# Attention and a gated layer on one core: eight of twelve column tiles and the last layer by seven-product blocks, with the gated values put into memory

## The chip, the cores and the metric

One core of a Trainium2 chip. The metric is the device time of one execution in microseconds (us), median of several runs.

## The reference, cut to what matters

Eight batches of linear attention (8 heads, 576 tokens, 64 wide, 128 random features) give 4608 tokens of 512 values; a gated layer of 1536 columns follows.

```python
h = x * scale @ omega.T - sq(x * scale) / 2
phi(x) = exp(h - max(h)) / sqrt(128)
num, den = phi(q) @ (phi(k).T @ v), phi(q) @ phi(k).sum()
x = (num / (den + 1e-6)) as [4608, 512]
out = (sigmoid(x @ w_gate) * (x @ w_val)) @ w_out    # 512 -> 1536 -> 512
```

The weights come as float64, in pairs of 32-bit words, and are made into float32 on the chip.

## The kernel before, in words

Matrix products of the gated layer are made exact enough by three passes: each operand is split into a high and a low part (`split`, line 52: ScalarE copies x to the high part, line 54; VectorE or GpSimd subtracts, line 55), and three matmuls, low by high, high by low and high by high, add up in PSUM.

Attention is a list of tasks (norms, keys, queries of a head pair and a batch), six at a time, a step of each in turn (`attention`, line 457). Its last step for a group of tokens is a transpose `pxq` (line 431), a copy to `xs`, and a store to `xT` in memory. `ready(n)` says whether the first n tokens are through.

Weights: `from_float64` (line 58) takes six VectorE operations and a GpSimd add for 384 columns at a time. The first four column tiles of 128 (`first_weights`) are converted and split before the gated layers start; the other eight (`convert_weights`) are converted beside them and put into memory (`w32`), and read back and split after attention (`late_weights`, tiles `w`, `wh`, `wl`).

The gated layers (`passes`, `gated`) are a second stream of pieces that runs beside attention, eight steps of attention per piece. There are two passes over all tokens. The first has four column tiles and chunks of 256 tokens: `gate` and `val` are products of 12 matmuls of 256 columns per tile (line 178, PSUM tiles `gv`), ScalarE takes the sigmoid (204), VectorE multiplies (207, tile `y`), `y` is split into `yh` and `yl`, and 128-token rows of it are multiplied with `w_out` into `acc` (line 192, 512 columns); `acc` is stored to `part`. The second pass has the other eight column tiles and chunks of 512 tokens, so its matmuls on line 178 have 512 columns; at a chunk's end `part` is read and added, and `out` stored.

Instructions are not issued in the order in which the code is written: the tile framework places them on each engine's queue by its own estimates and the code's order. Each queue then runs strictly in order. Matmuls run on PE; DVE is VectorE, ACT ScalarE, POOL GpSimd, SP the engine that issues most loads. Tile pools give each tag a fixed number of buffers, and a pool opened after another has closed takes its space and waits for its last users.

The core of the main loop, which the change rewrites:

```python
while not ready(B * S):
    next(gates)
    credit += RATE          # 8 steps of attention per piece
    while credit >= 1 and not ready(B * S):
        next(steps, None)
        credit -= 1
```

Of the kernel before, what the change touches and what calls it, by code (L numbers as in the profile page):

```python
# [17 lines left out]
M = 128  # L18
# [15 lines left out]
CA, CB = 256, 512   # tokens of a chunk of the gated layers, in their first and second pass  # L34
KC = DM // P
BANK = 512
NJ = DF // P
WP = 384            # weights converted at a time
NE = 4              # column tiles of the first pass
ACTIVE = {"n": 1, "k": 3, "q": 4}  # tasks of attention at a time: norms, keys, queries  # L40
AT_ONCE = 6         # tasks at a time
AHEAD = 8           # tasks to choose from
EVERY = 12          # steps of the first unit's attention per piece of weights
PUT = 5             # pieces of the gated layers per piece of weights
LATE = 3            # the same, once attention is through
# [3 lines left out]
WC = 2 * KC * P + DM   # weights of a column tile: gate, val, out  # L49


def split(nc, hi, lo, x, lo_engine=None):
    """x = hi + lo, both with the mantissa that one pass of the array carries."""
    nc.scalar.activation(out=hi, in_=x, func=AF.Copy)  # L54
    (lo_engine or nc.vector).tensor_tensor(out=lo, in0=x, in1=hi.bitcast(F32), op=ALU.subtract)  # L55
# [12 lines left out]
    # Patterns of positive numbers are in the numbers' order: exponents of -127 to 127 stay.  # L68
# [4 lines left out]
    # The sign and the exponent's highest bit stay in their places, three bits below them go.  # L73
# [7 lines left out]
    # The low word's 32 bits of the mantissa, in units of the number's power of two.  # L81
# [9 lines left out]
def attn_glu_kernel(ctx: ExitStack, tc, qT, kT, qn, kn, va, om, ident, w, out):  # L91
# [6 lines left out]
    w32 = dram.tile([NJ, P, WC], F32, name="w32")  # L98
    part = dram.tile([B * S, DM], F32, name="part")
# [9 lines left out]
    banks = {"at": 8 - 2 - CA // P, "gv": 2, "acc": CA // P}  # L109
# [12 lines left out]
    ws = [None] * NJ  # L122

    def pieces(pool, j):
        for i in range(WC // WP):
            s = slice(i * WP, (i + 1) * WP)
            raw = pool.tile([P, WP, 2], U32, tag="wraw", bufs=2, name=f"wraw{j}_{i}")
            nc.sync.dma_start(out=raw, in_=w[j, :, s, :])
            yield s, from_float64(nc, pool, raw, f"{j}_{i}", WP)

    def weights_of(pool, j):
        ws[j] = [pool.tile([P, WC], F32R, name=f"{n}{j}") for n in ("wh", "wl")]
        return ws[j]

    def first_weights(pool, temps, js):
        """Converts and splits column tiles' weights, a piece a step."""
        for j in js:
            wh, wl = weights_of(pool, j)
            for s, x in pieces(temps, j):
                split(nc, wh[:, s], wl[:, s], x, lo_engine=nc.gpsimd)  # L140
                yield

    def convert_weights(pool, js):
        """Converts column tiles' weights and puts them by, a piece a step."""
        for j in js:
            for s, x in pieces(pool, j):
                nc.sync.dma_start(out=w32[j, :, s], in_=x)
                yield

    def late_weights(pool, js):  # L150
        """Splits column tiles' weights that were put by, a piece a step."""
        n = WC // 2
        for j in js:
            wh, wl = weights_of(pool, j)
            for i in range(2):
                s = slice(i * n, (i + 1) * n)
                x = pool.tile([P, n], F32, tag="w32", bufs=2, name=f"w32_{j}_{i}")
                nc.sync.dma_start(out=x, in_=w32[j, :, s])
                split(nc, wh[:, s], wl[:, s], x)
                yield  # L160

    def gated(pool, C, c, x, js, first):
# [35 lines left out]
        for group in groups:  # L198
            if group is groups[-1]:
                yield True  # L200
# [286 lines left out]
    with tc.tile_pool(name="a", bufs=1, side="right") as pool:  # L487
# [10 lines left out]
        for _ in conv:  # L498
            pass
# [76 lines left out]
```

## Time and profile before

| what | value |
|---|---|
| median of 3 runs | 1295.61 us (1294.84 to 1296.29) |
| span of the profiled execution | 1296.1 us |
| PE busy, share of the span | 96% |
| DVE, ACT, POOL busy | 48%, 40%, 21% |
| bytes moved | 138.12 MB, mean 107 GB/s |
| start of the last `pxq` | 552.9 us |

A row of a group reads: line, engine, operation, output<-inputs, shapes, xcount, then busy us, mean ns of one, and the idle time of the engine before them with what ended it. PE's busy time of one matmul includes its way through the array, and neighbours overlap; what a matmul costs is the distance to the next. In rows of windows stand the stretch, its length, the busy time of each engine with the number of instructions, the granted TensorE clock, the DMA engines' share and GB/s. Rows of the chain of waits give start, length and what held the end then.

### The profile page before, as it was taken

What the parts mean: (1) busy time and instruction counts of PE and PEld (TensorE: products, weight loads), DVE (VectorE), ACT (ScalarE), POOL (GpSimd) and SP (SyncE); (2) the same over time, 40 slices, a digit from 0 to 9 for tenths busy, and PEclk for the clock granted to TensorE, in tenths of its full rate; (3) what the DMA queues carried; (4) which work ended last, traced back from release to release, by engine and by line L of the source; (5) the groups of instructions that cost most, each with busy time, mean ns of one, the idle gap of its engine ahead of it and who ended that gap; (6) DMA issues with size and microseconds to landing.
All of it is one profiled execution on the core that took longest, in us unless ns stands there. A gap on an engine that the chain in (4) does not pass through costs nothing.

```text
span 1296.1 us, 19491 instructions
## 1 busy us (share of the span) xinstructions
PE 1240.6 (96%) x7328; PEld 1077.6 (83%) x7328; DVE 620.0 (48%) x1445; ACT 520.4 (40%) x1119; POOL 276.3 (21%) x304
## 2 busy tenths in 40 slices
PE   5789989999999999999999999999999999999998
PEld 5778989898989988988998878787878787878786
DVE  6989899998988574634111121212121212121212
ACT  6556767676768656544222211112121212121111
POOL 4555253443432323011110100101010101010100
PEclk8779999999999999999999999999999999999999
DMA  8654677676755331154112020202020302020100
GB/s 272 203 178 139 183 228 242 186 241 212 221 174 171 103 119 52 50 178 140 51 49 81 1 98 1 98 1 98 1 98 1 98 1 98 1 98 1 60 6 33
DMA packets 76414, 138.12 MB, mean 107 GB/s; under 512 B 8480, under 2 KB 24096, under 8 KB 76320
## 3 DMA queue, kind: packets, MB, share of 16 engines
q1 hardware_dynamic: 49680, 97.67, 24.5%
q10 hardware_dynamic: 26640, 39.20, 8.8%
q8 instruction: 58, 0.95, 0.3%
q14 instruction: 36, 0.29, 0.1%
HBM read 102.24 MB, written 34.60 MB: 106 GB/s over the span
## 4 chain that ended last, share of the span: by engine, by line
PE 73%; DVE 16%; issue 5%; DMA 4%; ACT 2%; POOL 0%; SPq 0%; DVEq 0%; POOLq 0%; ACTq 0%
PE gv L178 41%; PE acc L192 18%; PE pnq L414 4%; PE pkv L371 4%; PE ptq L402 2%; DVE mxq L328 2%; DMA w<-w 2%; DVE yl L55 1%; DVE hq L391 1%; DVE mxk L328 1%; DVE f64t L78 1%; DMA wraw<-w 1%; DVE subq L389 1%; DVE hmq L331 1%; DVE f64a L84 1%
## 5 line engine op out<-in xcount | busy, mean ns | idle before, releaser
L178 PE MATMUL gv<-xh,wl 128*128 128x256 f32 (+1 forms) x1152 | 394.7, 343 | 1.7 <-POOL wl L55 1.3
L178 PE MATMUL gv<-xl,wh 128*128 128x256 f32 (+1 forms) x1152 | 394.1, 342 | 0.8 <-POOL xl L55 0.8
L178 PE MATMUL gv<-xh,wh 128*128 128x256 f32 (+1 forms) x1152 | 393.4, 342 | 0.0
L207 DVE TENSOR_TENSOR y<-gv,y 128x512 f32<-128x512 f32 x108 | 74.6, 690 | 490.6 <-PE gv L178 439.1
L178 PEld LDWEIGHTS gv<-xh,wl 128*128 128x128 f32 x1152 | 219.4, 191 | 29.8 <-POOL wl L55 1.7
L178 PEld LDWEIGHTS gv<-xl,wh 128*128 128x128 f32 x1152 | 219.3, 190 | 27.9 <-POOL xl L55 1.0
L178 PEld LDWEIGHTS gv<-xh,wh 128*128 128x128 f32 x1152 | 219.3, 190 | 26.7
L55 POOL TENSOR_TENSOR xl<-xr,xh 128x512 fp32r<-128x512 f32 (+1 forms) x76 | 95.6, 1273 | 643.4 <-ACT xh L54 607.4
L192 PE MATMUL acc<-wh,yl 128*128 128x512 f32 x432 | 174.3, 403 | 5.3 <-DVE yl L55 4.9
L204 ACT ACTIVATE y<-gv 128x512 f32<-128x512 f32 x108 | 64.6, 598 | 283.0 <-PE gv L178 262.9
L192 PE MATMUL acc<-wl,yh 128*128 128x512 f32 x432 | 172.7, 400 | 0.0
L192 PE MATMUL acc<-wh,yh 128*128 128x512 f32 x432 | 171.5, 397 | 0.0
L54 ACT ACTIVATE yh<-y 128x512 fp32r<-128x512 f32 x108 | 68.2, 631 | 229.3 <-DVE y L207 228.7
L55 DVE TENSOR_TENSOR yl<-y,yh 128x512 fp32r<-128x512 f32 x108 | 85.2, 789 | 58.9 <-ACT yh L54 58.9
L192 PEld LDWEIGHTS acc<-wh,yl 128*128 128x128 f32 x432 | 81.4, 188 | 27.4 <-DVE yl L55 10.4
L192 PEld LDWEIGHTS acc<-wh,yh 128*128 128x128 f32 x432 | 81.6, 189 | 18.0
L192 PEld LDWEIGHTS acc<-wl,yh 128*128 128x128 f32 x432 | 81.6, 189 | 16.5
L55 POOL TENSOR_TENSOR loq<-rawq,hiq 128x256 fp32r<-128x256 f32 (+1 forms) x80 | 59.4, 753 | 118.5 <-ACT hiq L54 118.4
L363 ACT ACTIVATE kpk<-ppk,nbk 128x128 f32<-128x128 f32 x256 | 72.9, 376 | 25.2 <-DVE nbk L352 22.9
L371 PE MATMUL pkv<-v,kpk 128*128 128x66 f32 x512 | 77.5, 288 | 4.5 <-ACT kpk L363 4.2
L371 PEld LDWEIGHTS pkv<-v,kpk 128*128 128x128 f32 x512 | 71.1, 206 | 8.0 <-ACT kpk L363 7.2
L414 PE MATMUL pnq<-kv,qpq 128*128 128x66 f32 (+1 forms) x640 | 75.8, 272 | 0.2 <-ACT qpq L404 0.2
(66 smaller groups left out, 1679.8 us busy)
## 6 DMA issues: line engine op xcount, KB each, us to landing
wraw<-w SPq DMA_DIRECT2D x48, 384.0 KB, 3.7
xr<-xT SPq DMA_DIRECT2D x68, 256.0 KB, 4.0
v<-va ACTq DMA_DIRECT2D x32, 330.0 KB, 3.9
natk<-kn SPq DMA_DIRECT2D x36, 256.0 KB, 4.4
natq<-qn SPq DMA_DIRECT2D x36, 256.0 KB, 3.7
part<-o ACTq DMA_DIRECT2D x36, 256.0 KB, 2.5
o<-part SPq DMA_DIRECT2D x36, 256.0 KB, 3.5
out<-o ACTq DMA_DIRECT2D x36, 256.0 KB, 3.8
```

The lines of the kernel that those rows point to most:

```text
L54: nc.scalar.activation(out=hi, in_=x, func=AF.Copy)
L55: (lo_engine or nc.vector).tensor_tensor(out=lo, in0=x, in1=hi.bitcast(F32), op=ALU.subtract)
L78: nc.vector.scalar_tensor_tensor(out=t, in0=hi, scalar=0xC0000000, in1=t, op0=ALU.bitwise_and, op1=ALU.bitwise_or)
L178: nc.tensor.matmul(gv[:, g * C : (g + 1) * C], lhsT=a[:, o : o + P], rhs=x[k], start=(m == 0), stop=(m == 3 * KC - 1),)
L192: nc.tensor.matmul(acc[t], lhsT=a[:, s], rhs=b[:, o : o + DM], start=(j == js[0] and m == 0), stop=(j == js[-1] and m == 2),)
L204: nc.scalar.activation(out=y, in_=gate, func=AF.Sigmoid)
L207: nc.vector.tensor_tensor(out=y, in0=val, in1=y, op=ALU.mult)
L328: nc.vector.tensor_reduce(out=mx, in_=pp, axis=AX.X, op=ALU.max)
L363: nc.scalar.activation(out=kp[t][:, h, :], in_=pp[:, 2 * i + h, :], func=AF.Exp, bias=nb[:, i, h : h + 1], scale=SCALE,)
L371: nc.tensor.matmul(pkv[:, h, :], lhsT=kp[b * MID + i][:, h, :], rhs=v[:, i, h, :], start=(i == 0), stop=(i == MID),)
L402: nc.tensor.transpose(out=pt[:, i, :], in_=h_sb[:, i, :], identity=id_sb)
L414: nc.tensor.matmul(pn[r, 2 * i + h, :], lhsT=qp[:, 2 * i + h, r], rhs=kvs[u, p, bb][:, h, :], start=True, stop=True,)
```

## The change

The first pass keeps four plain column tiles (`NE = 4`), now with chunks of 512 tokens (`NC`), and its gated values `y` go to memory (`ye`) without being multiplied with `w_out`. Attention has 12 steps per piece instead of 8, gated pieces begin at 512 tokens ready instead of 256, and one piece of 512 weight columns is converted per two gated pieces.

The other eight column tiles are taken as four pairs, and the products are done by a scheme of seven block products in place of eight: tokens in halves of 256 (Q), inner dimension in halves of two tiles, columns in halves of one tile. The columns `x` get four sums (`operands`: two from loads, four by VectorE and split like the rest, seven in all), and each pair's gate and val weights one `unit` of seven blocks (four from memory, `b`; four differences, `t`, of which VectorE makes each with one subtraction of 256 columns; then two splits, 768 and 1024 columns). `gated` then does for each of two kinds (gate, val) seven products of six matmuls of 256 columns (line 303, PSUM tiles `gw`) into three half-used banks; later products add onto earlier ones in the same bank, after a copy (`p1`) or an add (`u2`, `u3`) has read them. The last two products of a group are issued behind the first three of the next. GpSimd makes the seven operands of the last layer from the four gated blocks (seven operations of 256 columns), and they are stored to `yl`.

The last layer (`last`) comes after all chunks: for each of 18 blocks of 2 x 128 tokens, six pairs are loaded (four of 448 KB from `yl`, two from `ye`, for which VectorE makes the sums), split and multiplied: seven products of three matmuls of 256 columns (line 398, `po`, four banks), then seven adds and two stores. Its six units, n = 8 to 13, are made in the last chunk of the second pass and behind it, through the one buffer tagged `xr`, which the loads of `x` use too.

The diff, cut to its core:

```diff
-CA, CB = 256, 512
+NC = 512
+Q = NC // 2
-RATE = 8
+RATE = 12
+PRODUCT = {1: (0, 0), 2: (1, 1), 3: (6, 2), 4: (2, 6), 5: (3, 3), 6: (4, 4), 7: (5, 5)}
...
+    def unit(pool, n, at=None):
+        if at is None:
+            both = keep.tile([P, KC, NC], F32, tag="xr", bufs=1, name=f"wbt{n}")
+            b, t = both[:, :2], both[:, 2:]
...
+        nc.sync.dma_start(out=b, in_=w32[n])
+        u = pool.tile([P, 2, N_OPS, Q], F32R, tag="u", bufs=UL if pool is late else UE, name=f"u{n}")
+        for o, x, y in (
+            (t[:, 0], b[:, 3], b[:, 0]),
+            (t[:, 2], b[:, 2], b[:, 3]),
+            (t[:, 1], b[:, 2], t[:, 0]),
+            (t[:, 3], b[:, 1], t[:, 1]),
+        ):
+            nc.vector.tensor_tensor(out=o, in0=x, in1=y, op=ALU.subtract)
+        split(nc, u[:, 0, :3], u[:, 1, :3], b[:, :3])
+        split(nc, u[:, 0, 3:], u[:, 1, 3:], t)
...
+    def operands(c):
+        raw = load(c)
...
+        put(0, a11, nc.gpsimd)
+        s1 = combined(3, a21, a22, ALU.add)
+        s2 = combined(4, s1, a11, ALU.subtract)
+        put(4, s2)
+        put(3, s1, nc.gpsimd)
+        put(1, a12)
+        put(6, combined(6, a12, s2, ALU.subtract), nc.gpsimd)
+        put(5, combined(5, a11, a21, ALU.subtract))
+        put(2, a22)
...
+    def gated(c, x, pair, kind, g, y):
...
+        product(1, b0, True)
+        nc.scalar.activation(out=p1, in_=v0, func=AF.Copy)
+        product(6, b1, True)
+        add(u2, v1, p1)
+        product(5, b2, True)
+        yield
+        product(2, b0, False)
...
+        product(7, b1, False)
+        add(u3, v1, p1)
+        add(to[3], v2, u3)
+        yield
+        product(4, b1, False)
+        add(to[2], v1, p1)
+        product(3, b2, False)
+        add(to[1], v2, u2)
...
+    def last(c, s):
+        po = [any_bank(f"po{i}_{id_}") for i in range(4)]
...
+        for j in range(NPAIR):
+            t, n = (("y", 2 * N_OPS), ("g", 8))[j % 2]
+            raw = keep.tile([P, n, P], F32, tag=t, bufs=2, name=f"yr{id_}_{j}")[:, :8]
...
+            split(nc, yh, yl_, raw[:, :N_OPS], nc.gpsimd if j == NPAIR - 1 else None)
+            wh, wl = units[2 * (NPAIR - EP) + j]
+            for n, o in at.items():
+                i, k = PRODUCT[n]
+                for m, (u, v) in enumerate(((yl_, wh), (yh, wl), (yh, wh))):
+                    nc.tensor.matmul(
...
+        late = ctx.enter_context(tc.tile_pool(name="late", bufs=1, side="right"))
+        for n in range(2):
+            unit(late, n, late)
+        first = operands(0)
...
```

How the queues stand now. On PE in the second pass, before (gate and val of one column tile in `gv`, each `x` tile with three matmuls, then the previous tile's `acc`; here the end of one tile's `acc` and the start of the next `gv`):

```order
L192 MATMUL acc_4_3_12865<-wh_8793,yl_7_13019 128x512
L192 MATMUL acc_4_3_12865<-wl_8794,yh_7_13018 128x512
L192 MATMUL acc_4_3_12865<-wh_8793,yh_7_13018 128x512
L178 MATMUL gv_9_0_13079<-xh_8_0_12769,wl_9058 128x512
L178 MATMUL gv_9_0_13079<-xl_8_0_12773,wh_9057 128x512
L178 MATMUL gv_9_0_13079<-xh_8_0_12769,wh_9057 128x512
```

And after, at the turn from chunk 0 to chunk 1 (the names give kind, pair and chunk, then the bank's own number; `xl` is an operand, `u` a unit):

```order
L303 MATMUL gw_0_2_1_8514<-xl_4_8433,u_7582 128x256 x6
L303 MATMUL gw_0_2_1_8515<-xl_3_8436,u_7582 128x256 x6
L303 MATMUL gw_1_5_0_8440<-xl_2_7779,u_8170 128x256 x6
L303 MATMUL gw_1_5_0_8441<-xl_6_7734,u_8170 128x256 x6
L303 MATMUL gw_0_2_1_8513<-xl_1_8495,u_7582 128x256 x6
L303 MATMUL gw_0_2_1_8514<-xl_5_8505,u_7582 128x256 x6
L303 MATMUL gw_1_2_1_8576<-xl_0_8426,u_7594 128x256 x6
L303 MATMUL gw_1_2_1_8577<-xl_4_8433,u_7594 128x256 x6
L303 MATMUL gw_1_2_1_8578<-xl_3_8436,u_7594 128x256 x6
L303 MATMUL gw_0_2_1_8514<-xl_2_8508,u_7582 128x256 x6
```

Groups of six narrow matmuls have taken the place of the wide ones, a bank such as 8514 is written three times, with 18 to 24 matmuls between, and no `acc` stands among them.

On PE at the end of attention, before, around its last `pxq`:

```order
L192 MATMUL acc_0_1_7850<-wh_455,yl_0_7973 128x512
L192 MATMUL acc_0_1_7850<-wl_456,yh_0_7972 128x512
L431 MATMUL pxq_3_7_8206<-id_sb,xq_3_7_8204 128x128 x2
L192 MATMUL acc_0_1_7850<-wh_455,yh_0_7972 128x512
L192 MATMUL acc_0_0_7849<-wh_941,yl_2_8435 128x512
```

And after, 29 rows behind the last `pxq` and on, where chunk 7 of the first pass has just ended; `gv` with `xe_0_7799` is the start of chunk 8:

```order
L303 MATMUL gw_0_2_0_7982<-xl_4_7691,u_7582 128x256
L303 MATMUL gw_0_2_0_7981<-xl_0_7652,u_7582 128x256 x5
L303 MATMUL gw_0_2_0_7983<-xl_3_7694,u_7582 128x256 x6
L303 MATMUL gw_0_2_0_7982<-xl_4_7691,u_7582 128x256 x5
L303 MATMUL gw_0_2_0_7981<-xl_1_7729,u_7582 128x256 x6
L303 MATMUL gw_1_2_0_8035<-xl_4_7691,u_7594 128x256 x6
L303 MATMUL gw_1_2_0_8036<-xl_3_7694,u_7594 128x256 x5
L303 MATMUL gw_0_2_0_7982<-xl_5_7776,u_7582 128x256
L303 MATMUL gw_1_2_0_8036<-xl_3_7694,u_7594 128x256
L303 MATMUL gw_0_2_0_7982<-xl_5_7776,u_7582 128x256 x5
L303 MATMUL gw_0_2_0_7982<-xl_2_7779,u_7582 128x256 x6
L225 MATMUL gv_0_0_7811<-xe_0_7799,wl_111 128x512
```

Before, the first pass simply went on; now the second pass's first products stand on PE ahead of the first pass's last chunk.

On DVE behind attention's last `xq`, before (`wl`: late weights):

```order
L425 TENSOR_TENSOR xq_3_7_8204<-pnq_3_7_8195,invq_3_7_8202 128x256
L55 TENSOR_TENSOR wl_8439<-w_4_0_8440,wh_8438 128x768
L207 TENSOR_TENSOR y_0_8505<-gv_0_1_8507,y_0_8505 128x512
L55 TENSOR_TENSOR wl_8439<-w_4_1_8474,wh_8438 128x768
L55 TENSOR_TENSOR yl_0_8534<-y_0_8505,yh_0_8533 128x512
```

And after, the later part of it (`wt` and `u`: unit 1; `s` and `xl`: operands of second-pass chunk 0 from its load `xr_0_7603`):

```order
L194 TENSOR_TENSOR wt_7592<-wb_7591,wt_7592 128x256
L70 TENSOR_TENSOR u_7594<-wb_7591,u_7594 128x768
L194 TENSOR_TENSOR wt_7592<-wb_7591,wt_7592 128x256
L70 TENSOR_TENSOR xl_4_7691<-s_4_7657,xl_4_7691 128x512
L70 TENSOR_TENSOR xl_1_7729<-xr_0_7603,xl_1_7729 128x512
L264 TENSOR_TENSOR s_6_7732<-xr_0_7603,s_4_7657 128x512
L70 TENSOR_TENSOR u_7594<-wt_7592,u_7594 128x1024
L264 TENSOR_TENSOR s_5_7774<-xr_0_7603 128x512
L284 TENSOR_TENSOR u_2_0_7985<-gw_0_2_0_7982,p_2_0_7984 128x256
L70 TENSOR_TENSOR xl_5_7776<-s_5_7774,xl_5_7776 128x512
L70 TENSOR_TENSOR xl_2_7779<-xr_0_7603,xl_2_7779 128x512
```

The weights' preparation is longer, and the operands that hold `xr` stand behind it.

More of the change, by code (lines that the diff above doesn't have):

```diff
@@ L120, in any_bank @@
         return bank(cycle[-1], name)
[L122 to L133, printed above, removed]
@@ L249, in passes @@
[L249 to L268 removed]
+    ws = {}
@@ new lines, in attn_glu_kernel, with piece, first_weights @@
+    units = {}
+    def piece(pool, i):
+        raw = pool.tile([P, WP, 2], U32, tag="wraw", bufs=2, name=f"wraw{i}")
+        nc.sync.dma_start(out=raw, in_=w[:, i * WP : (i + 1) * WP, :])
+        return from_float64(nc, pool, raw, str(i), WP)
+    def first_weights(pool, temps):
+        n = WE // WP
+        for j in range(NE):
+            ws[j] = wh, wl = [pool.tile([P, WE], F32R, name=f"{t}{j}") for t in ("wh", "wl")]
+            for i in range(n):
+                s = slice(i * WP, (i + 1) * WP)
+                split(nc, wh[:, s], wl[:, s], piece(temps, j * n + i), lo_engine=nc.gpsimd)
+                yield
@@ new lines, in attn_glu_kernel @@
+    tail = ctx.enter_context(tc.tile_pool(name="tail", bufs=1))
+    cycle[:] = ["at", "at", "at", "gv"]
+    n = UL
+    for c, pair in second_pass(x):
+        if n < UL + UE:
+            unit(tail, n, keep)
+            n += 1
+        elif c == NCH - 1 and pair > EP and n < 2 * (NPAIR - EP) + 2 * (pair - EP):
+            unit(late if n < 2 * (NPAIR - EP) + UL else tail, n)
+            n += 1
+    while n < N_LATE:
+        unit(tail, n)
+        n += 1
+    for c in range(NCH):
+        for s in range(Q // P):
+            for _ in last(c, s):
+                pass
```

398 lines of the change are left out of this document (238 added, 160 removed).

## Prediction

> **What bounds the kernel now.** I read the page's totals and slices first, then the windows on both sides of the last attention matmul, then the chain of waits.
>
> ```profile
> span 1296.1 us, 19491 instructions
> PE 1240.6 (96%) x7328; PEld 1077.6 (83%) x7328; DVE 620.0 (48%) x1445; ACT 520.4 (40%) x1119; POOL 276.3 (21%) x304
> PE   5789989999999999999999999999999999999998
> PEclk8779999999999999999999999999999999999999
> ```
>
> TensorE (PE) is busy in nearly every slice, at full granted clock after the first tenth. The reader should see that no other engine is above half. The last attention matmul is a transpose `pxq`; the windows are cut there, for all engines, then for the matmuls of lines 178 and 192 alone:
>
> ```profile
> L431 PE MATMUL pxq<-id_sb,xq x144: 270/273/421, 53.6 to 552.9; 128*128 128x128 f32 x144
> 0.00:553.00 553.00, 506.61 (x3884) 474.99 (x3884) 450.88 (x1221) 362.35 (x866) 214.21 (x257) 0.96 0.56 175
> 553.00:1296.10 743.10, 733.95 (x3447) 602.65 (x3445) 169.15 (x224) 158.09 (x253) 62.06 (x47) 1.00 0.17 56
> 0.00:553.00 553.00, 155.12 (x1056) 136.61 (x1056) 0.96 0.56 175
> 0.00:553.00 553.00, 73.58 (x252) 43.23 (x252) 0.96 0.56 175
> ```
>
> Columns are PE, PEld, DVE, ACT, POOL. Until 553 us attention runs, with PE 92% and VectorE (DVE) 82% busy, so both count. After it PE is 99% busy and DVE 23%. What a matmul really costs there is read from the chain, since busy times of single matmuls overlap (start us, us, what):
>
> ```profile
> 574.98 6.07 DMA w<-w
> 582.94 3.85 DMA w<-w
> 612.66 11.51 PE gv L178 x96
> 692.71 2.79 PE acc L192 x12
> 695.50 5.61 PE gv L178 x24
> 744.75 1.54 DVE yl L55
> 812.67 1.54 DVE yl L55
> 1286.63 5.62 PE acc L192 x24
> ```
>
> The 96 matmuls of 256 columns (first pass) take 11.51/96 = 0.120 us each; those of 512 columns take 5.61/24 = 0.234 us. Halving a matmul's columns thus costs only 0.240 against 0.234 us for the pair, 2.5%. A chunk of the second pass takes 812.67 - 744.75 = 67.9 us for 288 x 0.234 = 67.4 us of matmuls: 0.5 us lost per chunk.
>
> **The change, part by part.** The sum is made against the profiled execution, 1296.1 us of span; no other time of that execution is given, and the median is 1295.6, so 0.5 is taken off at the end.
>
> *Matmuls of the gated layers.* Before: 1728 x 0.120 + (1728 + 1296) x 0.234 = 207 + 708 = 915 us. After: first pass 864 x 0.234 = 202; second pass 9 chunks x 4 pairs x 2 kinds x 42 = 3024 x 0.120 = 363; last layer 18 blocks x 6 pairs x 21 = 2268 x 0.120 = 272. Sum 837, 78 us less. An eighth of the two large parts goes; the halved width gives a fifth of that back, and the wider first pass takes 5 us off.
>
> *Until attention ends.* Attention's instructions stay. Before, 1056 x 0.120 + 252 x 0.234 = 186 us of gated matmuls stand before the last `pxq`; after, the order has 728 of L225's 512-column matmuls there, 170 us: PE 16 us less. On DVE and ScalarE (ACT), within these 553 us:
>
> ```profile
> L78 DVE SCALAR_TENSOR_TENSOR f64t<-wraw,f64t 128x384 uint32<-128x384 uint32 x48 | 30.2, 630 | 0.2
> L67 DVE TENSOR_SCALAR f64a<-wraw 128x384 uint32<-128x384 uint32 x48 | 18.4, 384 | 4.7 <-DMA wraw<-w 3.0 <-POOL loq L55 1.6
> L55 DVE TENSOR_TENSOR yl<-y,yh 128x512 fp32r<-128x512 f32 x22 | 16.0, 728 | 1.7 <-ACT yh L54 1.7
> L207 DVE TENSOR_TENSOR y<-gv,y 128x512 f32<-128x512 f32 x22 | 15.1, 685 | 14.4 <-PE gv L178 14.2 <-ACT qpq L404 0.2
> L204 ACT ACT_TABLE_LOAD x22 | 28.2, 1283 | 0.9 <-ACT xsq L437 0.4
> L54 ACT ACTIVATE yh<-y 128x512 fp32r<-128x512 f32 x22 | 13.9, 631 | 14.4 <-DVE y L207 13.8 <-DVE xq L425 0.6
> ```
>
> The six conversion operations (these two are the longest and the shortest) take 2.91 us per 384 columns, 48 times: 139 us. As 36 pieces of 512 they take between 105 (no growth with width) and 139 (proportional); I take 133. `yl` goes (-16), `y` is done 30 times instead of 22 (+6): DVE some 16 us less. ACT loses 22 `yh` (-14) and the copies of `acc`, and gains 16 table loads of 1.28 us (+20): about level. So the end of attention moves by 10 to 16 us: 540 us. Bounds: 528, if the emptier PE lets DVE run closer, and 560, if ACT's table changes sit in attention's chains.
>
> *The turn from first to second pass.* This is the new weak place. Behind the last attention matmul PE has 40 matmuls of chunk 7 (9.4 us) and 46 of the second pass (5.5 us), and then waits for chunk 8's operands. Their load needs the single `xr` buffer, which second-pass chunk 0 holds until its operands are split, and these go into space that attention frees only at its end. Rows for it:
>
> ```profile
> L425 DVE TENSOR_TENSOR xq<-pnq,invq 128x256 f32<-128x256 f32 x64 | 26.6, 416 | 0.5
> L55 POOL TENSOR_TENSOR xl<-xr,xh 128x512 fp32r<-128x512 f32 x68 | 89.2, 1329 | 638.0 <-ACT xh L54 602.0 <-issue 28.5 <-DMA xr<-xT 7.3
> L55 POOL TENSOR_TENSOR lok<-rawk,hik 128x256 fp32r<-128x256 f32 x64 | 48.7, 772 | 67.9 <-ACT hik L54 55.4 <-PE ppk L325 8.3 <-DMA natq<-qn 2.4
> L55 DVE TENSOR_TENSOR yl<-y,yh x108: 660/692/1752, 106.2 to 1288.1; 128x512 fp32r<-128x512 f32 x108
> L55 DVE TENSOR_TENSOR wl<-w,wh x16: 944/959/1889, 559.8 to 604.7; 128x768 fp32r<-128x768 f32 x16
> L207 DVE TENSOR_TENSOR y<-gv,y x108: 661/692/694, 103.4 to 1286.7; 128x512 f32<-128x512 f32 x108
> xr<-xT SPq DMA_DIRECT2D x68, 256.0 KB, 4.0
> out<-o ACTq DMA_DIRECT2D x36, 256.0 KB, 3.8
> ```
>
> After attention's last `xq`, 21 DVE rows come up to the last split of chunk 0, 23 operations: ten of 512 columns (0.69), nine of 256 (0.42), two of 768 (0.96) and two of 1024 (1.23, the step from 512 to 768 added again), about 15 us, starting when the unit's load lands some 5 us after the end. Then 4.0 us for chunk 8's `xr`, and about 2 us for its first split (0.63 on ACT, 1.33 on POOL): PE could go on 26 us after the end and had work for 15. I take 11 us of wait, between 4 (the rows overlap) and 20.
>
> *Second pass.* Per chunk PE needs 336 x 0.120 = 40.3 us. DVE has 44 adds and products of 256 columns from PSUM, 18.3 us, and eight of 512 columns, 5.5 us: 24 us, hidden, with 16 us left. GpSimd (POOL) has 28 operations of 0.77 and three of 1.33: 26 us, against four of 1.33 per chunk before; hidden too, since only `yl`'s store waits for it. ACT has 23 operations, at most 15 us by `yh`'s 0.63. But DVE and POOL disturb each other where both work on SBUF:
>
> ```profile
> 568.36 4.75 POOL L55 TENSOR_TENSOR xl<-xr,xh 128x512 fp32r<-128x512 f32 x3 [37.00 <-ACT xh L54]
> 570.09 1.89 DVE L55 TENSOR_TENSOR wl<-w,wh 128x768 fp32r<-128x768 f32 x1 [0.74 <-ACT wh L54]
> 571.91 1.75 DVE L55 TENSOR_TENSOR yl<-y,yh 128x512 fp32r<-128x512 f32 x1
> ```
>
> Two DVE operations with both inputs in SBUF took 1.89 and 1.75 us here beside POOL, against medians of 0.96 and 0.69, while `y`, with one input in PSUM, never took over 0.694. So the 44 PSUM operations should hold their time, and only the eight of 512 columns stretch, to 14 us at the worst: still 32 of 40. The Trainium skill (GPSIMD Engine Reference, Specifications) says that GpSimd's SBUF interface is shared with VectorE and contends with Vector instructions with two SBUF inputs; this trace agrees, 1.75 against 0.69 us. It speaks against the change, which takes POOL from a tenth to two thirds of this pass.
>
> In chunk 0 DVE also makes units 2 to 7: each four subtractions of 0.42, and 0.96 and 1.23, 3.9 us. About five fall in the chunk: 24 + 19 = 43 us of 40.3, plus waits for POOL of up to a microsecond in a part of 30 operations. I take 10 us of PE wait (0 to 20). Later chunks: 0.5 us each as before, 5 in all.
>
> *Into the last layer.* Units 8 to 13 go one after another through the single `xr` buffer: load about 4 (rows 3.85 and 6.07 above, for fewer bytes), 3.9 on DVE, waits: 9 to 10 us each, from the first third of chunk 8 on. The sixth is ready about 60 us after that chunk's start and wanted at 40 + 5 x 2.5 = 53: 10 us (0 to 25).
>
> *Last layer.* Per block PE needs 126 x 0.120 = 15.1 us; DVE about 10.5 (five splits of 896 columns at 1.1, eight small adds of 0.25 or so, seven of 0.42), ACT about 7; loads and stores 2.9 MB, 191 GB/s. The first stage moved 217 GB/s at 0.69 of the DMA engines' time:
>
> ```profile
> 0.00:97.60 97.60, 70.08 (x413) 66.69 (x414) 80.04 (x203) 56.36 (x159) 51.44 (x66) 0.79 0.69 217
> ```
>
> So this fits, with four loads ahead; 0.2 us per block, 4 in all. The end is an add and the store, 5 us.
>
> **Sum:** 540 + 136 x 0.234 (32) + 363 + 272 = 1207; waits 11 + 10 + 5 + 10 + 4 and the end 5 make 45: 1252, less 0.5 and rounded: 1251 us, 3.4% faster.
>
> **Rivals.**
>
> *DVE becomes the bound of the second pass (slower).* Place: the in-order DVE queue, whose adds release the PSUM that the next products write. It has 52 operations and 16 us to spare per chunk, 0.32 us each. If PSUM operations stretched beside POOL by 0.6 us, a little over half of what `yl` did, a chunk would take 24 + 31 = 55 us: 9 x 15 = 132 us more, 1383. It ends slower once a chunk passes 45 us. For it: POOL is busy two thirds of this pass, which no stage of before shows. Against it: `y` at 661/692/694. 6%.
>
> *The last layer is bound by its loads (slower).* At 3.5 us per pair instead of 2.52, 108 pairs give 106 us more, 1357. For it: all loads stand in one queue, with 448 KB each. Against it: the 217 GB/s. 4%.
>
> *Short waits between products eat the gain (same).* A product that accumulates into a bank waits for the copy and add that read it. The order puts 18 to 24 matmuls, 2.2 to 2.9 us, between; the reading takes 0.8. If every one of the 72 groups lost 0.6 us all the same, 43 us more: 1294. 4%, with neighbours on both sides.
>
> *It does not do what it says:* the counts of seven products are in the order, so this is left out; that halved matmuls cost more than 0.120 because stationary operands change with each is excluded by the 96 in a row that also changed them each time.
>
> **How the numbers follow.** The forecast's mechanism has 86%, the rivals 14%. Its terms reach from 1207 + 4 + 5 + 5 + 2 + 5 - 12 = 1216 to 1251 + 20 + 9 + 10 + 15 = 1305, but not all together: 1226 to 1284 leaves out the last 10 us below, the last 20 above and the two slower rivals, and holds 8 in 10. A measurement of this kernel can tell about 0.2%, 2.6 us. Faster 0.88 (the mechanism and some of the last rival), same 0.02, slower 0.10.
>
> **What would show it.** Right: chunks of the second pass 40 to 42 us apart, blocks of the last layer 15.1 to 15.6 us, last `pxq` near 540 us, a PE gap of about 10 us behind it and another before the first `po`. Wrong: a DVE that is over 90% busy in the second pass with PE waiting for its adds; `po` matmuls waiting for `yr` loads; attention ending after 565 us; or matmuls of 256 columns spaced wider than 0.125 us.

## The result, and the profile after

The changed kernel took 1341.99 us (median of 4 runs, 1338.92 to 1347.18) against 1295.83 (4 runs beside it): a ratio of 1.0376, 95% interval 1.0343 to 1.0409. It became 3.4 to 4.1% slower; the forecast was 1251 us.

The page of the changed kernel, the same rows as of before (totals, busy tenths of PE and the granted clock in 40 slices):

```profile
span 1342.1 us, 23861 instructions
PE 1215.7 (91%) x8732; PEld 1132.1 (84%) x8732; DVE 915.1 (68%) x2053; ACT 602.8 (45%) x1216; POOL 498.2 (37%) x541
PE   5789989898999999989789988998999599999998
PEclk8677999898999899989999999998999799999999
```

PE has less work than before (1215.7 against 1240.6 us busy), but its row of nines has become a row of eights and nines, and the clock row beside it has eights too. So there is less for PE to do, but it now stands still in between. Windows cut at the stages' ends (PE, PEld, DVE, ACT, POOL busy, granted clock, DMA share, GB/s), then the row of `pxq` and the last `po` row of the chain:

```profile
0.00:577.20 577.20, 515.54 (x3305) 453.38 (x3305) 435.57 (x1135) 360.59 (x843) 214.90 (x240) 0.91 0.58 177
577.20:627.00 49.80, 43.03 (x187) 34.56 (x186) 24.37 (x36) 17.33 (x27) 11.31 (x8) 0.90 0.33 104
627.00:1053.00 426.00, 383.05 (x2977) 370.78 (x2976) 251.84 (x516) 117.66 (x218) 225.66 (x270) 0.96 0.29 109
1053.00:1071.50 18.50, 8.20 (x46) 7.73 (x44) 12.98 (x19) 7.21 (x8) 7.27 (x7) 0.71 0.50 173
1071.50:1342.10 270.60, 265.88 (x2226) 265.68 (x2226) 190.29 (x349) 100.01 (x121) 39.02 (x17) 1.00 0.59 183
```
```profile
L579 PE MATMUL pxq<-id_sb,xq x144: 270/272/476, 54.6 to 577.2; 128*128 128x128 f32 x144
```
```profile
1071.47 264.17 PE po L398 x2211
```

Against the forecast, stage by stage in us (the turn is the time from the last `pxq` to the last `gv`; the second pass is from there to the last `gw`):

| stage | forecast | measured | miss |
|---|---|---|---|
| attention's end | 540 | 577.2 | +37 |
| turn | 48.4 | 49.8 | +1 |
| second pass | 372.5 | 426.0 | +54 |
| wait before the first `po` | 10 | 8.7 | -1 |
| `po`, first to last | 276 | 275.4 | -1 |
| end | 5 | 5.0 | 0 |

Two terms hold the whole miss. In the second pass I took the distances between the starts of neighbouring matmuls: 2975 at the undisturbed 0.119 us make 355; 198 that came at about half the clock add 19; 54 distances of 0.3 to 3.5 us, the holes, add 52. The waits of that stretch (engine, line, what it waited for: us, times, longest):

```profile
ACT p L313 <- POOL yl L341: 67.0, 13, 6.0
ACT p L313 <- DVE gl L284: 38.2, 10, 5.5
PE gw L303 <- ACT p L313: 30.7, 31, 2.8
```

ScalarE's copy `p` reads PSUM and depends on no GpSimd result. One such place in order of time shows why it waits for one all the same:

```profile
834.36 0.72 POOL L341 TENSOR_TENSOR yl<-yl 128x256 f32<-128x256 f32 x1
835.11 0.33 ACTq L342 DMA_DIRECT2D yl<-yl  x1
835.56 0.38 ACT L313 ACTIVATE p<-gw 128x256 f32<-128x256 f32 x1 [4.60 <-POOL yl L341]
835.98 0.42 DVE L284 TENSOR_TENSOR u<-gw,p 128x256 f32<-128x256 f32 x1 [2.43 <-ACT p L313]
836.00 10.29 PE L303 MATMUL gw<-xl,u 128*128 128x256 f32 x84 [2.20 <-ACT p L313]
```

GpSimd ends the last block of `y`; at that moment ScalarE's queue (ACTq) issues the store of `yl`, which had stood at its head; then the copy, then the add, then the matmuls. The order of ScalarE's queue says the same:

```
L322 ACTIVATE gl_2_9150<-gw_0_3_2_9152 128x256
L342 DMA yl<-yl_2_9030 128x1792
L313 ACTIVATE p_3_2_9218<-gw_1_3_2_9215 128x256
```

That is theory A: the store holds the copies. For attention I had theory D, that the `ye` store on ScalarE holds attention's exponentials in the same way, and beside it the activation tables. In the part of attention behind 100 us, before and after (waits of DVE for the products `pnq`, and the windows):

```profile
DVE denq L419 <- PE pnq L414: 22.4, 29, 2.4
100.00:553.00 453.00, 434.12 (x3462) 405.90 (x3460) 368.44 (x1014) 305.13 (x705) 161.72 (x190) 1.00 0.53 166
```
```profile
DVE denq L567 <- PE pnq L562: 45.8, 33, 5.2
100.00:577.20 477.20, 445.08 (x2908) 387.37 (x2906) 357.31 (x949) 304.61 (x689) 165.81 (x185) 0.95 0.56 169
```

ScalarE is busy for the same 305 us, so it was not given more work; DVE waits longer, and the clock is 0.95 instead of 1.00. One place of after, ScalarE's rows but for one of DVE and one of PE:

```profile
260.37 0.68 DVE L243 TENSOR_TENSOR ye<-gv,ge 128x512 f32<-128x512 f32 x1
261.08 0.90 ACTq L247 DMA_DIRECT2D ye<-ye  x2
261.16 0.38 PE L550 MATMUL ptq<-id_sb,hq 128*128 128x128 f32 x2
262.03 0.39 ACT L552 ACTIVATE qpq<-ptq 128x256 f32<-128x256 f32 x1 [2.77 <-PE ppq L471]
```

ScalarE stood idle for 2.77 us before the exponential `qpq`. The row names a matmul, but `qpq` starts as soon as the two `ye` stores are issued, and these as soon as DVE has made `ye`. Its own operand `ptq` was also late, though, made from 261.16 to 261.54: at this place the stores cost at most half a microsecond. The rows show the order in the queue; what it costs, the edits below must show.

### The profile page after: what moved, and what is told of

Read it like the earlier page. It is cut to its first block, busy times and chain, and to the rows that moved or that the text cites. A ratio compares the mean times of both kernels' runs of the same rounds, so it can differ in the third digit from the quotient of the medians.

```text
span 1342.1 us, 23861 instructions
## 1 busy us (share of the span) xinstructions
PE 1215.7 (91%) x8732; PEld 1132.1 (84%) x8732; DVE 915.1 (68%) x2053; ACT 602.8 (45%) x1216; POOL 498.2 (37%) x541
## 5 line engine op out<-in xcount | busy, mean ns | idle before, releaser
L303 PE MATMUL gw<-xl,u 128*128 128x256 f32 x3024 | 393.3, 291 | 47.8 <-ACT p L313 30.7
L303 PEld LDWEIGHTS gw<-xl,u 128*128 128x128 f32 x3024 | 379.4, 196 | 61.9 <-ACT p L313 37.9
L398 PE MATMUL po<-u,yh 128*128 128x256 f32 x1512 | 273.0, 283 | 0.0
L398 PEld LDWEIGHTS po<-u,yh 128*128 128x128 f32 x1512 | 235.4, 191 | 0.0
L398 PE MATMUL po<-u,yl 128*128 128x256 f32 x756 | 214.4, 284 | 10.3 <-DVE yl L70 10.3
L225 PE MATMUL gv<-xe,wh 128*128 128x512 f32 x576 | 195.8, 412 | 2.8 <-POOL xe L70 1.9
L69 ACT ACTIVATE yh<-yr 128x896 fp32r<-128x896 f32 x108 | 100.1, 950 | 153.0 <-PE po L398 68.1
L398 PEld LDWEIGHTS po<-u,yl 128*128 128x128 f32 x756 | 144.7, 191 | 10.8 <-issue 8.5
L225 PEld LDWEIGHTS gv<-xe,wh 128*128 128x128 f32 x576 | 108.1, 194 | 25.4 <-POOL xe L70 8.0
L225 PE MATMUL gv<-xe,wl 128*128 128x512 f32 x288 | 119.9, 420 | 5.3 <-ACT xe L69 3.6
```

The source lines that it names most:

```text
L225: nc.tensor.matmul(gv, lhsT=u[:, o : o + P], rhs=v, start=(m == 0), stop=(m == 3 * KC - 1))
L303: nc.tensor.matmul(o, lhsT=u[:, k, s], rhs=v[:, kc, :], start=(first and m == 0), stop=(m == 5), skip_group_check=not first,)
L398: nc.tensor.matmul(o, lhsT=u[:, i, :], rhs=v[:, k, :], start=(j + m == 0 and n in (1, 6, 5, 4)), stop=(j == NPAIR - 1 and m == 2), skip_gr ...
```

## The experiments

All edits are to the changed kernel. "Second pass", "holes" and "slow" are measured as above, in us, from each profiled run; "median" is of the timed runs. The kernel before took 1294.9 to 1295.5 beside them (medians of 7 to 17 runs). Five kernels (the changed one, `yl_sp`, `units_x`, `yl_pool`, `behind_only`) have the same order of instructions in every queue until attention has ended, and yet its end lies between 569 and 579; six others (those with the `ye` stores on SP and the sigmoid kept) have another common order, and it lies between 541 and 553. So in that column differences of some 10 us say nothing.

| kernel | median | attention's end | second pass | holes | slow |
|---|---|---|---|---|---|
| changed kernel | 1342.0 | 577 | 426 | 52 | 19 |
| `yl_sp` | 1336.6 | 571 | 420 | 47 | 18 |
| `ye_sp` | 1319.1 | 547 | 427 | 54 | 19 |
| `no_sigmoid` | 1314.2 | 537 | 429 | 54 | 19 |
| `units_x` | 1337.9 | 576 | 429 | 55 | 19 |
| `yl_pool` | 1331.4 | 579 | 411 | 43 | 13 |
| `ye_sp_yl_pool` | 1300.8 | 544 | 412 | 45 | 12 |
| `ye_sp_no_sigmoid` | 1306.5 | 534 | 425 | 55 | 15 |
| `yl_behind` | 1268.9 | 547 | 380 | 18 | 7 |
| `hold` | 1266.5 | 553 | 373 | 12 | 6 |
| `hold_units_x` | 1260.1 | 545 | 378 | 18 | 5 |
| `behind_only` | 1293.2 | 569 | 382 | 20 | 7 |
| `behind_hold_units_x` | 1265.6 | 541 | 379 | 17 | 7 |

### The store of `yl` on SP (`yl_sp`)

```diff
-        nc.scalar.dma_start(out=yl[pair - EP, :, c], in_=y)
+        nc.sync.dma_start(out=yl[pair - EP, :, c], in_=y)
```

> The stores of yl are issued by SP instead of ACT; nothing else is edited. Theory A (a store on ACT waits for GpSimd's seventh operation, and the copies p behind it on ACT hold PE): the 67 us that ACT stood before copies until GpSimd was done go, PE's waits in the second pass fall from 52 us to 20 or less, the clock there stays at 1.0, the second pass takes 370 to 385 us instead of 426, and the time is 1285 to 1302. Rival B (VectorE and GpSimd hold each other up on SBUF): no change of more than 10 us, 1332 to 1345. Rival C (the waits lie between products whatever ACT does): 10 to 15 us less, 1325 to 1332.

1336.58 us (ratio to before 1.0326, 1.0294 to 1.0358). The copies no longer wait for GpSimd, and yet the second pass is only 6 us shorter. The waits of that stretch, then rows of PE, SP and DVE at one chunk's border:

```profile
PE gw L303 <- DVE u L284: 36.1, 16, 5.4
DVE s L264 <- DMA xr<-xT: 29.7, 7, 5.8
```
```profile
832.80 26.76 PE L303 MATMUL gw<-xl,u 128*128 128x256 f32 x223
840.26 10.69 SPq L342 DMA_DIRECT2D yl<-yl  x2
849.32 0.68 DVE L70 TENSOR_TENSOR xl<-xr,xl 128x512 fp32r<-128x512 f32 x1
851.13 2.62 SPq L203 DMA_DIRECT2D xr<-xT  x4
858.10 1.20 DVE L264 TENSOR_TENSOR s<-xr 128x512 f32<-128x512 f32 x1 [3.68 <-DMA xr<-xT]
```

Within the pairs PE now runs 223 matmuls without a hole. But the first sum `s` of the next chunk now waits for its load at the head of DVE's queue, in front of the adds that TensorE needs. That load stands behind the store on SP and is issued at 851.13 us. The store is only a small part of its delay: the row of `xl` is the last that reads the old `xr`, and it ends at 850.00, so the load could not have come more than 1.1 us earlier, as in six of the seven chunks. One long hole per chunk has taken the place of several short ones. Theory A is half shown: the store held the copies, but taking it away lays open a wait that it does not cause.

### The stores of `ye` on SP (`ye_sp`)

```diff
-                    nc.scalar.dma_start(out=ye[j // 2, :, c, :, b], in_=y[:, i])
+                    nc.sync.dma_start(out=ye[j // 2, :, c, :, b], in_=y[:, i])
```

> The stores of ye in the first pass are issued by SP instead of ACT. Theory D (the store waits on ACT for the val product and VectorE's multiplication, and attention's exponentials stand behind it): attention ends at 555 to 567 us instead of 577, and the time falls by as much, to 1318 to 1332. Rival E (it is the changes of ACT's table that lengthen attention): the end of attention stays within 5 us of 577, the time at 1336 to 1345.

1319.13 us (1.0196, 1.0161 to 1.0231). Attention ends at 547 instead of 577, earlier than theory D expected (555 to 567); the second pass is unchanged. The six kernels with this order end attention at 541 to 553, the five without it at 569 to 579, so the edit's effect is clear. But the scheduler also put many of attention's rows in another order, so the 30 us are those of the edit, not of the wait alone.

### The first pass without its sigmoid (`no_sigmoid`)

```diff
-                nc.scalar.activation(out=flat, in_=gate, func=AF.Sigmoid)
+                nc.scalar.activation(out=flat, in_=gate, func=AF.Copy)
```

> The first pass's sigmoid is left out: ACT copies the gate instead, so the output is another one. No change of ACT's table is then needed beside attention (60 loads of 1.28 us go, 77 us of ACT). Rival E: attention ends 15 to 30 us earlier, at 547 to 562, and the time is 1312 to 1327. Theory D, or a third one in which PE's own pieces of 512 columns delay attention: less than 8 us, 1334 to 1345.

1314.17 us (1.0153, 1.01 to 1.0206). Attention ends at 537. The table loads (62 of 1.283 us before the edit) are down to 2, and ScalarE's busy time between 100 us and attention's end falls from 305 to 230 us. So the changes of tables weigh about as much as the stores, in this edit's order of rows.

### The last layer's units through other buffers (`units_x`)

```diff
-            both = keep.tile([P, KC, NC], F32, tag="xr", bufs=1, name=f"wbt{n}")
-            b, t = both[:, :2], both[:, 2:]
+            b, t = (buffer(f"{x}{n}", F32) for x in ("wb", "wt"))
```

> Units 8 to 13 are loaded into pairs of the 13 x buffers instead of the single xr buffer. If the single buffer makes the wait before the last layer, the gap of 8.7 us before the first po and the 2.3 us behind it go, and the end of the second pass loses some of its waits: 8 to 15 us less, 1327 to 1334. If VectorE's work on the units makes it, less than 5 us: 1337 to 1344.

1337.92 us (1.031 to 1.0373): in the profile the first `po` starts 6.9 us behind the last `gw` instead of 8.7. At most 2 us of this turn hang on the single buffer here. DVE's queue shows other waits; the first two rows are from the last chunk, the other two from the turn:

```profile
1050.89 0.29 DVE L386 TENSOR_TENSOR yr<-yr 128x128 f32<-128x128 f32 x1 [3.71 <-DMA yr<-ye]
1052.84 2.93 PE L302 MATMUL gw<-xl,u 128*128 128x256 f32 x12 [3.86 <-DVE u L283]
1061.02 2.09 DVE L70 TENSOR_TENSOR yl<-yr,yh 128x896 fp32r<-128x896 f32 x2 [2.12 <-ACT yh L69]
1062.25 0.55 PE L397 MATMUL po<-u,yl 128*128 128x256 f32 x1 [6.49 <-DVE yl L70]
```

In the last chunk a sum for the last layer waits for its load, and an add of the second pass stands behind it. In the turn the first `po` waits for the split `yl` on DVE, and this one for ScalarE's half of the split.

### The store of `yl` on GpSimd (`yl_pool`, `ye_sp_yl_pool`)

```diff
-        nc.scalar.dma_start(out=yl[pair - EP, :, c], in_=y)
+        nc.gpsimd.dma_start(out=yl[pair - EP, :, c], in_=y)
```

> Second pass: the store of yl is issued by GpSimd, right behind the operation that makes its last block, so neither ScalarE's copies p nor SP's load of xr stand behind it. Theory A (what held the second pass was whatever stood in a queue behind that store: on ScalarE the copies p, in the run with the store on SP the next chunk's xr): waits of TensorE between the first and the last gw fall from 52 to under 20 us, matmuls at a slow clock from 19 to under 10 us, the second pass from 426 to about 385, the total from 1342 to about 1302 (1290 to 1312); the rows of p no longer name POOL. Rival E (the hand-over through PSUM itself, product, copy, add, next product, is too tight, and the store was only the last of several waits): waits stay over 40 us under other names, the total at 1330 to 1340. Rival F (issuing the store costs GpSimd more than it has to spare): yl operations of GpSimd come later and later, the total over 1340.

> Both stores off ScalarE: ye on SP as in the earlier run (attention's end 577 to 547), yl on GpSimd. Theory A and D (the two passes lose their time independently of each other): 1342 less 23 less 40 = 1279 us (1268 to 1290), faster than the kernel before (1295). Rival E: about 1315, slower than the kernel before.

The first alone took 1331.38 us (1.028, 1.0262 to 1.0298), with the `ye` stores on SP as well 1300.79 (1.0046, 1.0019 to 1.0073). Both are some 20 to 30 us over what theory A expected: the second pass went from 427 to 412, not to 385. By its numbers the first run is rival E's (here the hand-over through PSUM: 1330 to 1340, over 40 us of holes); but E's holes would stand between the products of every group, and here the matmuls within the pairs run through. No copy waits for GpSimd, and the 45 us that are left have other names. The second one's waits between 597 and 1008 us, then two rows of DVE in one chunk:

```profile
PE gw L303 <- DVE u L284: 36.2, 18, 3.7
DVE s L264 <- DMA xr<-xT: 24.4, 7, 4.9
DVE s L264 <- POOL xl L70: 21.2, 7, 3.2
```
```profile
785.76 0.69 DVE L264 TENSOR_TENSOR s<-xr 128x512 f32<-128x512 f32 x1 [3.32 <-DMA xr<-xT]
794.80 0.69 DVE L264 TENSOR_TENSOR s<-xr,s 128x512 f32<-128x512 f32 x1 [2.99 <-POOL xl L70]
```

Twice in each chunk a sum for the next chunk stands in DVE's strict queue before its operand is there: the scheduler put the first one seven rows behind the last reading of `xr`, while the load into that buffer lands later (no store stands in front of the load here, and the wait is nearly that of `yl_sp`, 24.4 us for 29.7); the third needs a buffer that a GpSimd split still holds. That is theory J, tested below.

### Both causes of attention's delay taken away (`ye_sp_no_sigmoid`)

The edits of `ye_sp` and `no_sigmoid` together.

> First pass with its ye stores on SP and the sigmoid of its four column tiles left out (a copy stands in its place, so no activation table is changed for it; the second pass keeps its sigmoid). Alone the first edit moved attention's end from 577 to 547, the second to 537. Theory G (store and table changes are two separate charges on ScalarE's queue): they add, attention ends at 505 to 520, the total at about 1290. Theory H (both only make ScalarE late against the same partner, and with either gone VectorE's own work sets the pace): attention ends at 530 to 538, total about 1312.

1306.49 us, attention's end at 534: 30 and 40 us do not add to 70 but to 43. That is theory H in its numbers: the two charges overlap, and with either gone something else soon sets the pace. What that is was not looked into. So no fixed share of the 37 us can be given to the store or to the tables.

### The store one row later (`yl_behind`)

The `ye` stores are on SP; the `yl` store stays on ScalarE, but is issued only when the next pair's val group has been begun, and tied behind that group's copy:

```diff
-        nc.scalar.dma_start(out=yl[pair - EP, :, c], in_=y)
+        stores.append((yl[pair - EP, :, c], y))
...
+                    if kind and stores:
+                        o, t = stores.pop()
+                        store = nc.scalar.dma_start(out=o, in_=t)
+                        tc.add_manual_dep(store.ins, copied[0], info, reason="order")
```

ScalarE's queue then reads:

```
L322 ACTIVATE gl_2_9150<-gw_0_3_2_9152 128x256
L313 ACTIVATE p_3_2_9217<-gw_1_3_2_9214 128x256
L365 DMA yl<-yl_2_9030 128x1792
```

> The ye stores are on SP, and the yl store stays on ScalarE's queue, but stands one row later in it: behind the copy p of the next pair's val group instead of in front of it. Nothing else is moved. Theory A (the store's place in front of the copy is the wait): p no longer waits for GpSimd, and the second pass takes about the 411 us that it took with the store on GpSimd, against 427 with the store in front; the total goes from 1319 to about 1302. Rival I (it was a matter of ScalarE issuing the store at all, or of the store's traffic): the second pass stays at about 427, the total at 1319.

1268.85 us, 2.0% faster than the kernel before (ratio 0.9796, 0.9777 to 0.9815). The windows of the second pass and the sums' waits for `xr`, with the store in front of the copy (`ye_sp`) and behind it:

```profile
599.30:1026.70 427.40, 382.13 (x2977) 370.74 (x2976) 250.36 (x515) 116.75 (x218) 223.64 (x269) 0.96 0.29 108
DVE s L264 <- DMA xr<-xT: 10.0, 7, 2.1
```
```profile
599.30:979.00 379.70, 365.52 (x2977) 359.31 (x2977) 249.92 (x514) 115.59 (x216) 224.87 (x269) 0.99 0.32 120
DVE s L264 <- DMA xr<-xT: 7.3, 7, 2.6
```

The work is the same on each engine; 48 us of holes and slow matmuls are gone. Rival I is out. The gain is larger than theory A had expected, because its 411 us came from the kernel with the store on GpSimd, where the sums `s` waited 24.4 us for `xr` and 21.2 for a split. Here they wait 7.3 and 1.1, hardly less than with the store in front of the copy (10.0 and 0.7), so the sums explain little of the 48 us. The expectation was also wrong that nothing else moves: the scheduler put some of the pairs' adds a row or two elsewhere in DVE's queue, and what these moves give was not separated from the store's row.

### The sums held back in DVE's queue (`hold`, `hold_units_x`)

To `ye_sp_yl_pool` is added that the first and third sum for a chunk may not stand in front of a named add of the chunk before; `hold_units_x` has the edit of `units_x` as well.

```diff
+HOLD = {3: (2, 1), 6: (3, 1)}
...
+            inst = nc.vector.tensor_tensor(out=s, in0=a, in1=b, op=op)
+            if n in HOLD:
+                after(inst.ins, (c - 1, *HOLD[n]))
...
+        marks[c, pair, kind] = add(to[1], v2, u2).ins.name
```

> ye stores on SP, yl stores on GpSimd, and two rows per chunk moved later in VectorE's queue: the first sum for the next chunk (s, behind the last add of the pair two's val group of this chunk instead of some 5 rows behind the last reading of xr) and the third one (behind the same add of pair three). Theory J (what is left of the second pass's waits, 45 us, is VectorE's strict queue: per chunk s waits 3.3 us for the load of xr and 3.0 us for a GpSimd split that holds its buffer, and the adds that TensorE needs stand behind): the two rows of s no longer name xr or POOL, waits of TensorE in the second pass fall from 45 to under 12 us, the slow matmuls from 12 to under 6, the second pass to 365 to 378 us, the total from 1301 to 1262 (1255 to 1272), faster than the kernel before. Rival E (the PSUM hand-over is too tight anyway): waits over 30 us, total over 1285. Rival K (operands come too late for the next chunk if they start later): waits move to chunk borders on ACT xl or POOL xl, total 1275 to 1300.

> The kernel of the run hold, and the last layer's six units are loaded through pairs of the x buffers instead of the single xr buffer. In the changed kernel this alone moved the turn into the last layer by 2 to 4 us. Theory L (in the last chunk VectorE's subtractions for a unit wait for its load in front of the adds that TensorE needs, so more buffers for the loads help once the other waits are gone): 4 to 10 us less than hold. Rival M (VectorE's and ScalarE's work on the units itself is the limit): within 2 us of hold.

`hold` took 1266.54 us (0.9773, 0.9749 to 0.9797), `hold_units_x` 1260.11 (0.9734, 0.9704 to 0.9765). Theory J holds: the sums' rows no longer name `xr`, and POOL only once (0.9 us); a stretch of PE in `hold` reads

```profile
779.83 50.40 PE L313 MATMUL gw<-xl,u 128*128 128x256 f32 x422
```

more than a chunk without a hole, 0.119 us per matmul. The rivals' PSUM hand-over and late operands are out. With more buffers the wait before the first `po` is shorter (5.8 us for 10.6), but the second pass is longer (378 for 373). Between the two kernels the profile shows 1.8 us from the last `gv` to the end (663.0 against 661.2); the rest of the difference stands in attention, whose queues the edit does not touch, and the runs overlap (1261 to 1270, 1256 to 1269). Whether the buffers help is left open.

### One edit alone, and all that helped (`behind_only`, `behind_hold_units_x`)

The first is the changed kernel with only the store's edit of `yl_behind`; the second is `hold_units_x` with that edit instead of the store on GpSimd.

> The changed kernel with one edit: the yl store stands one row later in ScalarE's queue, behind the copy p of the next pair's val group; the ye stores stay on ScalarE too. Theory A (that one row is the larger part of what the change lost): the second pass falls from 426 to about 380 us, attention stays at about 577, the total falls from 1342 to about 1292 (1285 to 1300), level with the kernel before or a little faster. Rival N (the gain of the earlier run needed the ye stores off ScalarE too, since attention's delay and the second pass's are one): total over 1320.

> ye stores on SP, yl stores on ScalarE behind the next pair's copy, the two sums held back in VectorE's queue, the last units loaded through the x buffers: all the edits that helped, with ScalarE's store instead of GpSimd's. Theory A and J: the second pass takes 365 to 375 us, the total is 1250 to 1260. Rival O (the store on ScalarE was better than on GpSimd only because it also moved other rows): 1260 to 1268, no better than with GpSimd.

`behind_only` took 1293.15 us, level with the kernel before (1.0003, 0.9979 to 1.0027) and 49 us less than the changed kernel, as theory A said (1292). In its profile 44 us of this are the second pass's (382 for 426). The rest is in the main attention's end, 569 for 577, on queues that are the same up to there, so the store's place, with the small moves of DVE's rows that come with it as in `yl_behind`, is worth some 44 us. `behind_hold_units_x` took 1265.55 (0.978, 0.9747 to 0.9813), no better than with GpSimd and in the range of rival O (1260 to 1268): once DVE's rows are right, these runs show no difference between the two engines. The best version remains `hold_units_x`, 2.4 to 3.0% faster than the kernel before.

## Why the prediction was wrong

**Second pass, 372 against 426: the failed step.** "hidden too, since only `yl`'s store waits for it" asked who waits for GpSimd and stopped at the store. It did not ask what is queued behind the store on ScalarE: the copy `p` of the next pair, behind it the add, behind that the product that writes the same bank. `behind_only` puts 44 of the 54 us on that place. The step also took DVE's 24 us per chunk as hidden because 16 were left, and did not ask where in its queue the sums stand; in the changed kernel they waited some 13 us, in `ye_sp_yl_pool` 46. With the store's wait and the two sums out of the way (`hold`) the pass takes 373 us, and its holes and slow matmuls come to 18 us where I had 15.

**Attention, 540 against 577: the failed step.** "about level" was true of ScalarE's busy time (305 us each) and said nothing of when its operations come. DVE had its 15 us less, as forecast (435.6 for 450.9 up to the end), and it did not help; the sign "attention ending after 565 us" came. The 560 us bound named the tables; the stores on ScalarE, each waiting for a product of DVE, were not priced at all. The six kernels with `ye` on SP and the sigmoid kept end attention between 541 and 553 us, at the forecast or up to 13 us behind it; leaving the sigmoid out gave 537. So the stores, which the step put at nothing, and the tables, which it had in its bound alone, both count; they overlap, and how the 37 us divide stays open.

**What held.** Two numbers held by luck. The turn took 49.8 us, but not with the foreseen gap of some 10 us in front of chunk 8: PE was idle for 6.8 us in pieces of at most 2.44, the longest in front of the second pass's products, 1.6 of it before chunk 8's `gv`, and the clock was 0.90 meanwhile. The wait into the last layer was 8.7 for 10, but without the single buffer that it was reckoned from it was still 6.9 (`units_x`). The last layer held in its terms: 264.17 / 2211 = 0.1195 us per matmul, 183 GB/s, one hole of 2 us near its start. The width's price held as well: 0.119 to 0.120 us per matmul of 256 columns wherever PE had no hole and the full clock.

**The rivals.** *DVE as the bound* did not come: its PSUM operations kept their time beside a GpSimd that was busy for half of the pass, and DVE was busy for 59% of it. Rows by form:

```profile
L284 DVE TENSOR_TENSOR u<-gw,p x144: 408/425/427, 597.4 to 1050.0; 128x256 f32<-128x256 f32 x144
L284 DVE TENSOR_TENSOR yl<-gw,u x72: 404/424/428, 636.4 to 1056.9; 128x256 f32<-128x256 f32 x72
```

*The last layer bound by loads* did not come either. *Short waits between products* came closest, 43 us against 52, but by another mechanism: the 0.8 us of reading that I weighed against 2.2 to 2.9 us of matmuls was right, and the copy simply did not start. I gave it 4% because I priced the chain and not the queue that one of its links stands in.

## What to carry to other kernels

A store is an instruction of the engine that issues it: if its data come late, ask what stands behind it in that engine's queue, and who waits for that. Moving it to another queue passes the question on: on SP the next load stood behind it for about a microsecond per chunk, and on either queue the next wait, that of DVE's sums, took its place. Putting it one row later, behind the operation that others wait for, shortened the second pass by 44 us. In a strict queue a row that prepares the next chunk should stand where its operands are there for certain, not where a scheduler thinks they might be.

## What the runs showed of the hardware

**The queue, not the transfer.** Issuing `yl` takes 0.33 us on ScalarE and the transfer 3.6 us behind it, and still the store's place moved the second pass by 44 us. The Trainium skill (DMA: Bandwidth & Descriptors, Issuing engines are not separate DMA queues) says that issuing from several engines saves only the time to initiate the transfers, usually a small one. For the transfers these runs don't contradict it; the 44 us come from the wait in front of the issue, which that section doesn't price.

**The clock.** Holes cost more than their length. Windows of after behind the hole of 8.3 us in front of the first `po`, and a little later (PE busy, granted clock, DMA share, GB/s):

```profile
1061.60:1066.20 4.60, 4.50 (x21) 0.50 0.75 262
1071.50:1100.00 28.50, 28.50 (x239) 1.00 0.66 205
```

The 21 matmuls came 0.21 us apart at half the clock, the 239 later ones 0.119. Shorter holes did it too, though not each time: 18 matmuls took 3.73 us behind one of 2.37 us, while the 84 behind the hole of 2.20 us shown above took 10.29, near full clock.

```profile
1043.74 3.73 PE L303 MATMUL gw<-xl,u 128*128 128x256 f32 x18 [2.37 <-DVE u L284]
```

The clock's records show why. The granted clock changes only at steps of 3.41 us; windows cut at these steps, around the hole of 2.37 us and then around that of 2.20 (PE busy, granted clock, DMA share, GB/s):

```profile
1039.93:1043.34 3.41, 1.44 (x12) 1.00 0.16 37
1043.34:1046.75 3.41, 3.01 (x14) 0.50 0.72 286
831.72:835.13 3.41, 2.08 (x17) 1.00 0.00 0
835.13:838.55 3.42, 2.55 (x21) 1.00 0.68 273
```

The first hole left PE idle for 58% of one stretch, and the next had half the clock; the second hole fell across a step, and neither stretch was idle for half of its time. The second passes of the thirteen kernels have 1458 such stretches at full clock: all 58 that were idle for more than 57% were followed by one at half clock, of the 31 at 49 to 57%, ten were, and of the 1369 below, one. The Trainium skill (TensorE: Matmul & The Clock Gate, Part 1) says that a free-running window of some 3.4 us with an idle array halves the clock, and a busy one restores it. The steps of 3.41 us and the half clock agree; by these rows a stretch need not be idle throughout. In the second pass of the changed kernel the slow matmuls added 19 us to 52 us of holes, and both went together (7 and 18 in `yl_behind`).
